# VectorE's attention as a hardware loop, and 160 matmuls that reuse the weights already held

## The chip, the cores and the metric

One core of one Trainium2 chip. The metric is the device time of one execution in microseconds (us); the quoted number is the median of the fast runs. Runs in a slow state, over 1.5% above the fastest of the same kernel, are left out (for the kernel before these were 888.3 us once and about 444 us in single runs). The traces' own span is about 1.3 us shorter than the measured time.

## The reference, cut to what matters

```python
mod = (_silu(c) @ w_mod).reshape(c.shape[0], 6, 1, -1)       # six shifts, scales, gates
h = _layernorm(x, axis=-1) * (1 + ca) + sa
q = (h @ wq) ...                                             # 8 rows, 32 heads of 128
scores = einsum('bhqd,bhkd->bhqk', q, k) * Dh ** (-0.5)      # k_cache: 8 x 4 x 8192 x 128
o = einsum('bhqk,bhkd->bhqd', softmax(scores), v)            # v_cache: the same size
x = x + ga * (o @ wo)
h = _layernorm(x, axis=-1) * (1 + cb) + sb
x = x + gb * ((relu(h @ W_gate) * (h @ W_up)) @ W_down)
```

One token for each of 8 batch entries attends to 8192 cached keys and values. The two caches are 134 MB, and all inputs together about 186 MB. Each byte is used once, so this is a streaming kernel.

## The kernel before

The attention is 16 tiles (`M = 16`). A tile is one K and one V load of 4.19 MB each. The loads go through a ring in on-chip memory with room for four of them. A small scheduler records every operation with what it reads and writes, works out the waits, and emits one program per engine. TensorE's attention was already a hardware loop of 8 trips with two tiles each; VectorE's was written out 16 times.

```python
def pump():                              # issues the next load when its place in the ring is free
    while stream:
        key, src, n = stream[0]
        lo = cursor[0] if cursor[0] + n <= RING else 0
        if P.unread("arena", lo, lo + n):
            return
        ...
        P.op("sp", lambda e, dst=dst, src=src: e.dma_start(dst, src), writes=[slot_r(lo, lo + n)], dma=True, ...)

def qk_part(m, e8):                      # scores of an eighth of a tile: 4 matmuls
    ...
    P.op("pe", fns, reads=[R("kt", to, to + QE), R("qpad", ...), slot_r(place["k", m] + e8 * QE, ...)], writes=[bank(b)])

for m in range(M):
    P.trip = m // 2
    for e8 in range(8):
        kt_part(m, e8)                   # VectorE: transposes an eighth of K (ring of 4 results)
        qk_part(m, e8)                   # TensorE: scores of that eighth
        if e8 == 5:
            rowmax(m, 0)                 # VectorE: maximum of the first half
    make_qpad(m + 2)                     # GpSimd: padded queries for a later tile
    fold(m - 1, 0); fold(m - 1, 1)       # VectorE: gathers the output of the tile before
    rowmax(m, 1); spread(m); fold(m - 1, 2)
    headmax(m)                           # VectorE: maximum of each head -> bias
    expo(m)                              # ScalarE: exponentials
    fold(m - 1, 3); fold_pe(m - 1); ...
    p_turn(m)                            # VectorE: transposes the probabilities
    pv(m)                                # TensorE: 32 matmuls, probabilities times V
```

In the modulation, query, gate and up stages 4 column tiles (`tile_position=(0, 32 * j)`) multiply the same `hT[:, kk, :]` by two or three blocks of columns. Each matmul loaded these weights anew.

## Time and profile before

| | before |
|---|---|
| time, median of the fast runs | 437.71 us |
| span in the trace | 436.2 us |
| bytes moved | 185.63 MB |
| busy: TensorE, VectorE | 63%, 60% |
| weight loads | 1697 |

From the page of the kernel before: the busy row, then the share of the DMA engines and the GB/s in 40 equal slices of the span, then the load queue.

```profile
PE 273.5 (63%) x1697; PEld 124.0 (28%) x1697; DVE 263.0 (60%) x373; ACT 30.7 (7%) x65; POOL 20.9 (5%) x79
...
DMA  9999999999999999999999999999999999999995
GB/s 376 421 457 431 433 433 431 430 433 433 433 433 433 433 433 433 433 433 433 433 433 433 433 433 433 433 433 433 433 433 430 433 433 433 441 429 434 427 421 224
...
q1 hardware_dynamic: 6848, 185.63, 98.8%
```

The DMA engines are full in every slice but the last, at 433 GB/s. 185.63 MB at 433 GB/s are 428.7 us of the 436.2.

The chain that ended last in the kernel before, by engine and by line:

```profile
DMA 38%; PE 33%; DVE 20%; issue 8%; ACT 0%; SPq 0%
DMA arena<-in_A_k_cache_dram 25%; PE ps L594 13%; PE ps L550 12%; DVE kt L539 12%; DMA arena<-in_w_mod_dram 7%; DMA arena<-in_B_W_down_dram 6%; DVE negm L558 4%; PE ps L744 2%; PE ps L694 1%; PE ps L564 1%; PE ps L615 1%; DVE om L609 1%; DVE mj L569 1%; PE ps L725 1%; PE ps L463 1%
```

VectorE's longest wait in the kernel before (total us, times, longest):

```profile
DVE kt L539 <- DMA arena<-in_A_k_cache_dram: 37.9, 16, 3.1
```

And the load queue's own waits, for a place in the ring:

```profile
SPq L343 <- PE ps L594: 182.0, 16, 12.7
SPq L343 <- PE ps L550: 127.1, 16, 16.9
```

V's place is freed by the PV matmuls (L594), K's by the score matmuls (L550). How far ahead the loads run is in the last column of the issue lines (KB each, median us from issue to landing):

```profile
arena<-in_A_k_cache_dram SPq DMA_DIRECT2D x16, 4096.0 KB, 27.5
arena<-in_A_v_cache_dram SPq DMA_DIRECT2D x16, 4096.0 KB, 25.6
```

One such load takes 4.19 MB / 433 GB/s = 9.7 us, so at its issue there is a queue in front of it. The order of one tile in the timeline of the kernel before (start us, duration, engine, line, operation):

```profile
220.09 5.38 PE L550 MATMUL ps<-kt,qpad 128*128 128x512 bf16 x24
220.19 0.33 SPq L343 DMA_DIRECT2D arena<-in_A_v_cache_dram  x1
...
223.80 0.66 DVE L558 TENSOR_REDUCE negm<-ps 128x1 f32<-128x512 f32 x1
...
227.87 0.33 SPq L343 DMA_DIRECT2D arena<-in_A_k_cache_dram  x1
```

V's load goes out as soon as the PV matmuls end (220.19), and K's as soon as the last score matmul ends (227.87).

One stage with weight loads to be removed, the second query batch, as a window of the kernel before (window; busy us and count of PE, PEld, DVE, ACT, POOL; granted clock; DMA share; GB/s):

```profile
52.30:56.00 3.70, 3.60 (x32) 1.08 (x32) 0.00 (x0) 0.00 (x0) 0.00 (x0) 0.50 0.98 425
```

### The profile page before, as it was taken

Reading aid. Unit: us, or ns where it says so; the run is one execution under the profiler, and the core shown is the slowest. Engines: PE = TensorE matmul, PEld = TensorE weight load, DVE = VectorE, ACT = ScalarE, POOL = GpSimd, SP = SyncE. Lnnn points to the kernel's source line nnn. Section 1 sums busy time; section 2 is a strip of 40 time slices with the busy share of each in tenths; the row PEclk is TensorE's granted clock in tenths of the full one; section 3 lists DMA queues with packets and bytes.
Section 4 is the critical chain, followed back from the end, with each engine's and each line's share of the span. In section 5 each row is a group of like instructions: output and inputs, shape, how many; then the busy total and the mean of one; then the engine's idle time right before and its main releaser. Section 6 shows DMA issues by size and latency. Waiting matters only on the chain.

```text
span 436.2 us, 4054 instructions
## 1 busy us (share of the span) xinstructions
PE 273.5 (63%) x1697; PEld 124.0 (28%) x1697; DVE 263.0 (60%) x373; ACT 30.7 (7%) x65; POOL 20.9 (5%) x79
## 2 busy tenths in 40 slices
PE   0052447769595866859586775959586684655237
PEld 0021112324242332424233232423233231342015
DVE  0233057778596878778696877859686877332020
ACT  1100020010101011010101101010101101010000
POOL 7000010000000000000000000000000000000000
PEclk9996558698787989787896969879798978868568
DMA  9999999999999999999999999999999999999995
GB/s 376 421 457 431 433 433 431 430 433 433 433 433 433 433 433 433 433 433 433 433 433 433 433 433 433 433 433 433 433 433 430 433 433 433 441 429 434 427 421 224
DMA packets 6939, 185.79 MB, mean 426 GB/s; under 512 B 816, under 2 KB 912, under 8 KB 1168
## 3 DMA queue, kind: packets, MB, share of 16 engines
q1 hardware_dynamic: 6848, 185.63, 98.8%
q8 instruction: 6, 0.10, 0.1%
q10 hardware_dynamic: 80, 0.02, 0.0%
q14 instruction: 5, 0.04, 0.0%
HBM read 185.63 MB, written 0.02 MB: 426 GB/s over the span
## 4 chain that ended last, share of the span: by engine, by line
DMA 38%; PE 33%; DVE 20%; issue 8%; ACT 0%; SPq 0%
DMA arena<-in_A_k_cache_dram 25%; PE ps L594 13%; PE ps L550 12%; DVE kt L539 12%; DMA arena<-in_w_mod_dram 7%; DMA arena<-in_B_W_down_dram 6%; DVE negm L558 4%; PE ps L744 2%; PE ps L694 1%; PE ps L564 1%; PE ps L615 1%; DVE om L609 1%; DVE mj L569 1%; PE ps L725 1%; PE ps L463 1%
## 5 line engine op out<-in xcount | busy, mean ns | idle before, releaser
L539 DVE STREAM_TRANSPOSE kt<-arena 128x1024 uint32<-128x1024 uint32 x128 | 148.5, 1214 | 40.5 <-DMA arena<-in_A_k_cache_dram 37.9
L550 PE MATMUL ps<-kt,qpad 128*128 128x512 bf16 x512 | 122.0, 384 | 10.3 <-DVE kt L539 8.8
L594 PE MATMUL ps<-arena,pT 128*64 128x512 bf16 x512 | 92.0, 538 | 50.9 <-issue 50.9
L594 PEld LDWEIGHTS ps<-arena,pT 128*64 128x64 bf16 x512 | 44.2, 153 | 92.6 <-issue 86.7
L550 PEld LDWEIGHTS ps<-kt,qpad 128*128 128x128 bf16 x512 | 45.6, 97 | 85.2 <-DVE kt L539 29.6
L585 DVE STREAM_TRANSPOSE pT<-prb 64x1024 bf16<-64x1024 bf16 x32 | 39.7, 1239 | 16.8 <-ACT prb L578 16.3
L578 ACT ACTIVATE prb<-ps,bias 128x1024 bf16<-128x1024 f32 x16 | 17.8, 1114 | 286.5 <-DVE mjt L572 286.5
L558 DVE TENSOR_REDUCE negm<-ps 128x1 f32<-128x512 f32 x32 | 22.0, 688 | 11.3 <-PE ps L550 11.1
L532 POOL COPY qpad<-qR 32x32 bf16<-32x32 bf16 x64 | 13.0, 203 | 304.7 <-PE ps L550 252.0
L725 PE MATMUL ps<-arena,hT 128*32 128x448 bf16 x128 | 11.0, 515 | 13.6 <-DMA arena<-in_B_W_gate_dram 6.8
L564 PE MATMUL ps<-identf,negm 128*128 128x128 f32 x32 | 7.8, 326 | 15.6 <-DVE negm L562 15.6
L615 PE MATMUL ps<-jmp,om 128*128 128x16 f32 x34 | 6.7, 273 | 16.9 <-DVE om L609 16.1
L609 DVE SCALAR_TENSOR_TENSOR om<-ps,im,om 128x128 f32<-128x128 f32 x48 | 16.7, 347 | 0.6
L486 PE MATMUL ps<-arena,hT 128*32 128x512 bf16 x64 | 7.2, 631 | 14.1 <-DMA arena<-in_A_wq_dram 14.1
L732 DVE TENSOR_TENSOR kt<-ps,kt 128x448 bf16<-128x448 f32 x2 | 1.2, 620 | 23.5 <-PE ps L725 23.5
L744 PE MATMUL ps<-arena,hmT 128*32 128x256 bf16 x112 | 9.0, 332 | 5.3 <-DMA arena<-in_B_W_down_dram 5.3
L401 DVE CAST cxr<-ps 128x512 bf16<-128x512 f32 x1 | 0.7, 692 | 18.1 <-PE ps L399 18.1
L399 PE MATMUL ps<-cx,rsel 32*128 32x512 bf16 x1 | 0.6, 604 | 17.5 <-DMA cx<-in_c_dram 17.5
L564 PEld LDWEIGHTS ps<-identf,negm 128*128 128x128 f32 x32 | 4.7, 186 | 23.5 <-DVE negm L562 23.5
L496 DVE CAST kt<-ps 128x512 bf16<-128x512 f32 x1 | 0.7, 692 | 17.8 <-PE ps L486 17.8
L615 PEld LDWEIGHTS ps<-jmp,om 128*128 128x128 f32 x34 | 5.1, 188 | 20.3 <-DVE om L609 19.4
L725 PEld LDWEIGHTS ps<-arena,hT 128*32 128x32 bf16 x128 | 4.2, 128 | 20.1 <-DMA arena<-in_B_W_gate_dram 7.2
(89 smaller groups left out, 103.9 us busy)
## 6 DMA issues: line engine op xcount, KB each, us to landing
arena<-in_A_k_cache_dram SPq DMA_DIRECT2D x16, 4096.0 KB, 27.5
arena<-in_A_v_cache_dram SPq DMA_DIRECT2D x16, 4096.0 KB, 25.6
arena<-in_w_mod_dram SPq DMA_DIRECT2D x2, 6144.0 KB, 24.0
arena<-in_A_wq_dram SPq DMA_DIRECT2D x2, 4096.0 KB, 31.1
arena<-in_A_wo_dram SPq DMA_DIRECT2D x2, 4096.0 KB, 26.9
arena<-in_B_W_gate_dram SPq DMA_DIRECT2D x2, 3584.0 KB, 23.6
arena<-in_B_W_up_dram SPq DMA_DIRECT2D x2, 3584.0 KB, 24.6
arena<-in_B_W_down_dram SPq DMA_DIRECT2D x1, 3584.0 KB, 25.5
```

The costliest lines, as they stand in the source:

```text
L532: P.op("pool", lambda e, n=2 * m + Q // 2, Q=Q: e.tensor_copy(qpad[32 * Q:32 * Q + 32, m % 2, :, 24 + 32 * Q:32 + 32 * Q], qR[32 * Q:32 * ...
L539: P.op("dve", lambda e: e.transpose(ktb[:, to:to + QE].bitcast(dt.uint32), arena[:, lo:lo + QE].bitcast(dt.uint32)), reads=[slot_r(lo, lo ...
L550: fns.append(lambda e, t=t, r=r: e.matmul(ps[:, b, :].rearrange("p (c k) -> p c k", k=32), qpad[:, m % 2, t * 2 + r, 24 - 8 * i:152 - 8 * ...
L558: P.op("dve", lambda e: e.tensor_reduce(negm[:, h:h + 1], ps[:, b, :], AX.X, ALU.max, negate=True), reads=[bank(b)], writes=[R("negm", h, ...
L564: P.op("pe", lambda e: e.matmul(ps[:, 4, 0:128], negm[:, 2:3].to_broadcast([128, 128]), identf[:], start=True, stop=True), reads=[R("negm" ...
L578: P.op("act", lambda e: e.activation(prb[:], ps[:, 2 * z:2 * z + 2, :].rearrange("p h n -> p (h n)"), ACT.Exp, bias=bias[:, z:z + 1], scal ...
L585: P.op("dve", lambda e, g=g: e.transpose(pT[64 * g:64 * g + 64, z, :, g, :], prb[64 * g:64 * g + 64, :]), reads=[R("prb"), R("pT", z, z + ...
L594: fns.append(lambda e, t=t: e.matmul(ps[64 * (t % 2):64 * (t % 2) + 64, 5, :].rearrange("p (i d) -> p i d", d=Dh), pT[:, z, t].rearrange(" ...
L609: P.op("dve", lambda e, i=i: e.scalar_tensor_tensor(out=om[:], in0=ps[:, 5, Dh * i:Dh * i + Dh], scalar=im[:, i:i + 1], in1=om[:], op0=ALU ...
L615: P.op("pe", lambda e: e.matmul(ps[:, 6 + z, 0:16], om[:], jmp[:].rearrange("p g j -> p (g j)"), start=True, stop=True), reads=[R("om"), R ...
L725: fns.append(lambda e, w=w, r=kk - r0, kk=kk, h=h, j=j, b0=b0: e.matmul(ps[32 * j:32 * j + 32, b0 + h, 0:H], hT[:, kk, :], w[:, r, j, h, : ...
L744: fns.append(lambda e, w=w, r=k - r0, k=k, i2=i2, j=j: e.matmul(ps[32 * j:32 * j + 32, 4, 0:256], hmT[:, k, 1 - i2:33 - i2], w[:, r, i2, j ...
```

## The change

The intent is a shorter program for VectorE, and fewer weight loads on TensorE. A loop can only wait for counts that rise by the same amount on every trip, so the change also moves where a load finds out that its place is free. Its core, with cuts marked by `...`:

```diff
+    LOOPED = ("dve", "pe")
...
-                with nc.Fori(0, len(self.trips), engines=(mybir.EngineType.PE,)):
+        with nc.Fori(0, len(self.trips["pe"]), engines=tuple(kinds[x] for x in self.LOOPED)):
...
+def hold_weights(nc, held):
+    names = {x.ins.name for x in held}
+    for block in nc.main_func.blocks:
+        block.instructions = [copy.replace(x, ldweights=False) if x.name in names else x for x in list(block.instructions)]
...
-                            start=(kk == 0), stop=(kk == KC - 1), tile_position=(0, 32 * j)))
+                            start=(kk == 0), stop=(kk == KC - 1), tile_position=(0, 32 * j)), pr > 0))
... (the same for the query with z > 0, for gate and up with h > 0)
-            P.op("pe", fns, reads=[R("kt", to, to + QE), R("qpad", m % 2, m % 2 + 1), slot_r(place["k", m] + e8 * QE, ...)],
+            P.op("pe", fns, reads=[R("kt", to, to + QE), R("qpad", m % 2, m % 2 + 1)],
...
+        def free(*keys):
+            return [slot_r(*P.held.pop(key)) for key in keys if key in P.held]
...   (rowmax)
-                 reads=[bank(b)], writes=[R("negm", h, h + 1)])
+                 reads=[bank(b)] + (free(("v", m - 1)) if h == 0 else []), writes=[R("negm", h, h + 1)])
...   (headmax)
-                 reads=[R("mj"), R("jms")], writes=[R("mjt"), R("bias", z, z + 1)])
+                 reads=[R("mj"), R("jms"), R("qpad", z, z + 1)] + free(("k", m)), writes=[R("mjt"), R("bias", z, z + 1)])
...   (order of the tile)
-            make_qpad(m + 2)
             fold(m - 1, 0)
...
             headmax(m)
+            make_qpad(m + 2)
```

Two query copies also change places between VectorE and ScalarE. `fold(-1, ...)` now runs in the first tile instead of a memset, so that all trips are alike.

## The prediction

> **What bounds the kernel now.** The DMA stream. The page's 40 slices show the DMA engines at nine tenths or more in 39 slices and 430 to 433 GB/s nearly throughout attention. The DMA queues moved 185.63 MB: at 433 GB/s that is 428.7 us of a 436.2 us span; the rest is start-up (376 GB/s in the first slice) and the tail. The Trainium skill, "DMA: Bandwidth & Descriptors", section "Where 436 GB/s comes from", gives 435.2 GB/s as the ceiling of the 16 SBUF ports; the measured 433 agrees. TensorE (63% busy) and VectorE (60%) are not the limit, although the chain of waits names them (PE 33%, DVE 20%): in the list of waits VectorE waits 37.9 us for K tiles, 2.4 us in each of 16 half-trips.
>
> **Removed.**
> 1. 160 weight loads (64 modulation, 32 query, 64 gate/up), about 0.15 us each by the profile but overlapping matmuls: in the query stage (timeline, granted clock 0.50) four loads take 0.16 us in a pitch of 0.43 us, which the matmuls set. These stages shorten by at most 1 us together. All end before the next DMA lands; the tightest is up's second half, whose product is ready 2.3 us before the down weights land (422.4 against 424.7). On the critical path: 0.
> 2. VectorE's 16 half-trips of program text become 2 in a loop of 8. Executed instructions stay about 373.
>
> **Added or moved.**
> 1. A register update and compare-and-branch per trip on VectorE. Estimate 0.1 to 0.5 us a trip, before a transpose where VectorE waits 1.9 to 2.7 us for K anyway. "Runtime: NRT & Kernel Launch", "Instruction fetch mechanics", warns that a taken branch outside the fetch window stalls; TensorE's existing loop shows none (0.41 us before the first score matmul, at trip ends as within trips).
> 2. Loads wait for VectorE alone. K's slot is freed by the head-max step instead of the last score matmul: about 2 us later. V's is freed by the next tile's first row-max instead of the last PV matmul: 4.3 us later (220.2 to 224.5 in the timeline). Loads now land a median of 27.5 us (K) and 25.6 us (V) after issue, while 4.19 MB takes 9.7 us: 16 to 18 us of earlier transfers are still queued at issue. The delays eat slack; the stream stays unbroken. First tiles are tightest (about 8 us left). Issue-to-landing medians should fall to about 25.5 and 21.5 us, GB/s unchanged.
> 3. The query copies swap between VectorE and ScalarE; the first K lands 2.7 us after they end. GpSimd's padding copies start 2 us later, a whole tile before use.
>
> **On the critical path:** nothing. Start, stream and tail (last down tile, two VectorE operations, output DMA: about 3 us) are untouched.
>
> **Predicted: 437.6 us, 80% range 436.9 to 438.5.** Faster by over 2%: 1%; within 2%: 97%; slower by over 2%: 2%.
>
> **What would show each step right:** 433 GB/s in the attention slices; weight loads 1537, not 1697; VectorE's busy time within 1 us; the load queue waiting for VectorE lines instead of TensorE lines; V issue-to-landing about 4 us shorter; VectorE still waiting for K in most half-trips, its loop ends hidden there.
>
> **What would make it wrong:** an instruction-fetch stall of over 5 us at each of VectorE's loop ends (fetches share the saturated DMA engines); a late slot release that empties the queue, most likely at the first V reloads or the second gate tile (about 9 us of slack); a lower granted clock in the down projection, where TensorE is just ahead of the DMA (waits of 0.26 and 0.30 us), costing up to 1 us; matmuls without their load running slower than with it.

## The result, and the profile after

| | before | after |
|---|---|---|
| time, median of the fast runs | 437.66 us | 437.19 us |
| fast over fast | | 0.9987, 95% interval 0.9972 to 1.0002 |
| span in the trace | 436.2 us | 435.9 us |
| instructions in the trace | 4054 | 3952 |

A ratio is the mean time of one kernel's fast runs over the mean of the other's of the same rounds. It need not be the ratio of the medians, because a mean feels a single long run. The verdict is "same": 0.5 us between the medians, and an interval that just includes 1.

From the page of the kernel after, the lines shown of before:

```profile
PE 275.6 (63%) x1697; PEld 120.4 (28%) x1537; DVE 265.4 (61%) x376; ACT 30.7 (7%) x65; POOL 20.9 (5%) x79
...
DMA  9999999999999999999999999999999999999995
GB/s 367 435 447 436 432 433 433 432 430 433 433 433 433 433 433 433 431 433 433 433 433 433 433 433 433 433 431 433 433 433 433 433 433 433 426 433 444 421 425 233
...
q1 hardware_dynamic: 6848, 185.63, 98.9%
```

The same stream with the same 433 GB/s, and 160 weight loads fewer.

The chain that ended last in the kernel after:

```profile
PE 46%; DVE 20%; issue 13%; DMA 7%; ACT 0%; SPq 0%
PE ps L634 21%; PE ps L586 18%; DVE kt L575 9%; DMA arena<-in_B_W_down_dram 7%; DVE negm L598 5%; PE ps L604 2%; PE ps L651 2%; PE ps L762 1%; PE ps L731 1%; DVE om L645 1%; DVE mj L609 1%; DVE mjt L612 1%; DVE negm L602 1%; DVE kt L721 0%; DVE lx L693 0%
```

The chain's share of loads fell from 38% to 7%, while the time did not move. A chain that changes its face this much at equal time may mean that two limits lie side by side. It is weak evidence: the wait for K has another name in the kernel after (see below), and the chain of `loop_only`, which has the same loop and waits, adds up to only 18% of the span. The experiments below decide.

VectorE's wait for K in the kernel after. `DVEq` is VectorE's own sequencer: it waits for the load and counts its semaphore back down, so the wait is the former wait for K under another name.

```profile
DVE kt L575 <- DVEq L180: 30.6, 16, 2.8
```

The load queue's waits:

```profile
SPq L377 <- DVE negm L598: 204.4, 15, 14.4
SPq L377 <- DVE mjt L612: 94.8, 16, 19.2
```

The load issues:

```profile
arena<-in_A_k_cache_dram SPq DMA_DIRECT2D x16, 4096.0 KB, 25.0
arena<-in_A_v_cache_dram SPq DMA_DIRECT2D x16, 4096.0 KB, 20.7
```

And the same tile in the timeline of the kernel after:

```profile
221.15 5.38 PE L586 MATMUL ps<-kt,qpad 128*128 128x512 bf16 x24
...
224.84 0.69 DVE L598 TENSOR_REDUCE negm<-ps 128x1 f32<-128x512 f32 x1 [0.23 <-PE ps L586]
...
225.56 0.33 SPq L377 DMA_DIRECT2D arena<-in_A_v_cache_dram  x1
...
230.94 0.33 SPq L377 DMA_DIRECT2D arena<-in_A_k_cache_dram  x1
```

V's load now waits for the row maximum, 4.4 us after the PV matmuls end. K's waits for the head maximum. So loads land 2.5 us (K) and 4.9 us (V) sooner after their issue: less of a queue in front of them, and none of it lost to the stream.

The second query batch, as a window of the kernel after:

```profile
52.90:56.60 3.70, 3.60 (x32) 0.59 (x16) 0.03 (x1) 0.03 (x1) 0.00 (x0) 0.50 1.07 461
```

Half of the weight loads are gone, and the 32 matmuls take 3.60 us as before, at the same granted clock of 0.50. The loads had been hidden behind the matmuls.

### The profile page after: what moved, and what is told of

The parts are those of the page before. It is cut to its first block, busy times and chain, and to the rows that moved or that the text cites. A ratio compares the mean times of both kernels' runs of the same rounds, so it can differ in the third digit from the quotient of the medians.

```text
span 435.9 us, 3952 instructions
## 1 busy us (share of the span) xinstructions
PE 275.6 (63%) x1697; PEld 120.4 (28%) x1537; DVE 265.4 (61%) x376; ACT 30.7 (7%) x65; POOL 20.9 (5%) x79
## 4 chain that ended last, share of the span: by engine, by line
PE 46%; DVE 20%; issue 13%; DMA 7%; ACT 0%; SPq 0%
PE ps L634 21%; PE ps L586 18%; DVE kt L575 9%; DMA arena<-in_B_W_down_dram 7%; DVE negm L598 5%; PE ps L604 2%; PE ps L651 2%; PE ps L762 1%; PE ps L731 1%; DVE om L645 1%; DVE mj L609 1%; DVE mjt L612 1%; DVE negm L602 1%; DVE kt L721 0%; DVE lx L693 0%
## 5 line engine op out<-in xcount | busy, mean ns | idle before, releaser
L575 DVE STREAM_TRANSPOSE kt<-arena 128x1024 uint32<-128x1024 uint32 x128 | 149.6, 1217 | 36.8 <-DVEq L180 30.6
L586 PE MATMUL ps<-kt,qpad 128*128 128x512 bf16 x512 | 121.8, 384 | 9.5 <-DVE kt L575 8.2
L634 PE MATMUL ps<-arena,pT 128*64 128x512 bf16 x512 | 93.1, 543 | 50.8 <-issue 50.8
L625 DVE STREAM_TRANSPOSE pT<-prb 64x1024 bf16<-64x1024 bf16 x32 | 39.7, 1239 | 16.7 <-ACT prb L618 16.1
L598 DVE TENSOR_REDUCE negm<-ps 128x1 f32<-128x512 f32 x32 | 22.1, 692 | 12.2 <-PE ps L586 12.2
L568 POOL COPY qpad<-qR 32x32 bf16<-32x32 bf16 x64 | 13.1, 204 | 307.7 <-DVE mjt L612 254.3
L762 PE MATMUL ps<-arena,hT 128*32 128x448 bf16 x128 | 12.3, 570 | 10.8 <-DMA arena<-in_B_W_up_dram 5.5
L645 DVE SCALAR_TENSOR_TENSOR om<-ps,im,om 128x128 f32<-128x128 f32 x51 | 17.7, 347 | 0.7
L435 PE MATMUL ps<-cx,rsel 32*128 32x512 bf16 x1 | 0.6, 604 | 17.7 <-DMA cx<-in_c_dram 17.7
L781 PEld LDWEIGHTS ps<-arena,hmT 128*32 128x32 bf16 x112 | 6.0, 109 | 9.2 <-DMA arena<-in_B_W_down_dram 8.1
## 6 DMA issues: line engine op xcount, KB each, us to landing
arena<-in_A_v_cache_dram SPq DMA_DIRECT2D x16, 4096.0 KB, 20.7
```

The costliest lines, as they stand in the source:

```text
L568: P.op("pool", lambda e, n=2 * m + Q // 2, Q=Q: e.tensor_copy(qpad[32 * Q:32 * Q + 32, m % 2, :, 24 + 32 * Q:32 + 32 * Q], qR[32 * Q:32 * ...
L575: P.op("dve", lambda e: e.transpose(ktb[:, to:to + QE].bitcast(dt.uint32), arena[:, lo:lo + QE].bitcast(dt.uint32)), reads=[slot_r(lo, lo ...
L586: fns.append(lambda e, t=t, r=r: e.matmul(ps[:, b, :].rearrange("p (c k) -> p c k", k=32), qpad[:, m % 2, t * 2 + r, 24 - 8 * i:152 - 8 * ...
L598: P.op("dve", lambda e: e.tensor_reduce(negm[:, h:h + 1], ps[:, b, :], AX.X, ALU.max, negate=True), reads=[bank(b)] + (free(("v", m - 1)) ...
L625: P.op("dve", lambda e, g=g: e.transpose(pT[64 * g:64 * g + 64, z, :, g, :], prb[64 * g:64 * g + 64, :]), reads=[R("prb"), R("pT", z, z + ...
L634: fns.append(lambda e, t=t: e.matmul(ps[64 * (t % 2):64 * (t % 2) + 64, 5, :].rearrange("p (i d) -> p i d", d=Dh), pT[:, z, t].rearrange(" ...
```

## The experiments

Twelve kernels ran. All passed the comparison with the reference, also the four that are meant to compute something else: its tolerance doesn't notice their cuts, so passing says nothing about them.

### Which part moved the half microsecond

`hold_only` is the kernel before with only the weights held, `loop_only` the kernel after with every weight load put back, and `after_again` the kernel after unchanged. All ran on one chip in the same rounds.

```diff
  # hold_only: the kernel before, plus
+        hold_weights(nc, holding)          # and hold(...) around the matmuls of the four stages
  # loop_only: the kernel after, with
-        if when:
+        if False:
             holding.append(ins)
```

> The kernel before with only the weights held (160 loads fewer); VectorE straight, slots freed as before. The whole change came out about 0.5 us faster than before, less than 0.2 per cent. Theory A (instruction fetches: the traces show 6 fetches of 16 KB on one queue before and 5 after, 5 against 3 of 8 KB on another, each carried in 0.9 or 0.3 us, and loads land when the slowest DMA engine is done): 5 of the 16 KB fetches and 5 of the 8 KB fetches here, and most of the gain, 437.1 to 437.5 us. Theory B (the gain comes from the loop or the later slot release): no gain, 437.5 to 437.8. In both the time stays within 0.3 per cent of before, because the stream bounds it.

> The kernel after with all weight loads put back (1697 loads); VectorE's loop and the later slot release kept. Theory A: 6 fetches of 16 KB and 3 of 8 KB, so part of the gain at most, 437.3 to 437.7 us. Theory B: the whole gain, 437.0 to 437.3. V loads land about 21 us after issue as in the kernel after.

> The kernel after, unchanged, in the same rounds: 437.0 to 437.3 us, 0.3 to 0.6 us under before, as in the first measurement. If the difference from before is not there in these rounds, it was a matter of the day and nothing needs explaining.

| | time | ratio to before |
|---|---|---|
| before | 437.65 us | |
| hold_only | 437.58 us | 0.9978, 0.9923 to 1.0033 |
| loop_only | 436.86 us | 0.9966, 0.9917 to 1.0015 |
| after_again | 437.05 us | 0.9964, 0.9915 to 1.0013 |

Before had three fast runs of 438.3 to 444.0 us in these rounds, which widens all intervals; read the medians. Holding the weights gave nothing (0.07 us). The kernel with the loop alone gave all of it (0.8 us); it has the later release and the swapped query copies too. In theory A, the 16 KB fetches carried most of the gain. That falls: `hold_only` has one of them fewer in its trace (5 instead of 6) and is no faster. Theory B, the loop or what comes with it, stands. What comes with the loop are two fetches fewer of 8 KB (3 instead of 5 during the span). The next two runs ask whether such fetches can cost anything.

### Do instruction fetches cost the stream anything

`pool_pad` and `pool_pad_half` add 1200 and 600 one-element memsets at the end of GpSimd's program. GpSimd is idle then, and nobody waits for it.

```diff
+        padt = sb("padt", [128, 1200], dt.bfloat16)
+        for i in range(1200):              # 600 in pool_pad_half
+            P.op("pool", lambda e, i=i: e.memset(padt[0:1, i:i + 1], 0.0), writes=[R("padt", i, i + 1)])
         P.plan()
```

> The kernel after with 1200 one-element memsets added at the end of GpSimd's program, which is idle then and which nobody waits for: about 77 KB of instructions more to fetch, no other work. Theory A: the fetched bytes hold up one DMA engine of 16 (27 GB/s of 433), so 0.5 to 2.8 us longer than after. Rival (fetches cost only their bytes spread over all engines, 0.18 us, or nothing): within 0.3 us of after.

> Half the dose of the padding: 600 memsets on idle GpSimd, about 4 or 5 fetches of 8 KB more than in the kernel after instead of 9. 1200 cost 4.3 us, about 0.46 us a fetch. If each fetch holds up the one DMA engine that finishes last: 1.7 to 2.4 us over after, about 439.2 us. If the cost sits in something that comes once (another placement in memory, a threshold): 0 or 4 us. The stream's slices before the pads must stay the same.

`pool_pad` took 441.39 us, 4.3 us more than `after_again` in the same rounds. `pool_pad_half` took 438.16 us, about 1.1 us more than `after_again`, which ran on another chip (before read 437.65 us on both). The fast runs of each lie within 0.3 us. The traces count 12 fetches of 8 KB in `pool_pad`, 7 in `pool_pad_half` and 3 in the kernel after.

The DMA rows of `pool_pad` show where the time went:

```profile
DMA  9999999999999999999999999999999999999992
GB/s 408 439 395 429 427 441 450 437 429 429 429 429 429 429 435 429 436 447 441 432 429 429 432 429 429 429 436 432 447 441 433 427 427 427 437 419 429 446 407 89
```

Look at the last slice: 89 GB/s, where the kernel after had 233. Adding up the load packets of the trace in order of their ends, 184 MB had been moved after 427.5 us in the kernel after and after 427.7 us in `pool_pad`. But 185.6 MB took 432.2 and 436.1 us. So the bulk of the stream kept its pace, and a small rest of it came 3.9 us late. The last down tile's weights, and all output behind them, wait for that rest.

The packet and landing records of the traces show where the delay sits. While the stream runs, 16 load packets are in flight; during each added fetch there are 15. From 432.7 to 436.7 us, the end of `pool_pad`'s loads, there is one at a time, each starting as the last one ends, at first 8 KB in 0.31 us: about a sixteenth of 433 GB/s. Each load leaves 16 landing events, which I take as one per DMA engine (the trace does not name the engines). How late the last of the 16 is after the eighth:

| | last load before the pads | after all pads | last load of the stream |
|---|---|---|---|
| after | 1.98 us | 1.96 us | 1.84 us |
| pool_pad_half | 1.74 us | 2.97 us | 2.80 us |
| pool_pad | 2.07 us | 6.28 us | 6.10 us |

One engine fell back, and the others kept their pace. The last landing grew later by 1.2 and 4.2 us, the 1.1 and 4.3 us of the measured times. In `pool_pad` this engine was 3.01, 4.33, 5.63 and 6.28 us late after 4, 6, 8 and 9 of the added fetches, and in `pool_pad_half` 2.97 us after 4: 0.65 us a fetch in both. Reckoned back, it had been 0.4 us late before the pads, while another engine was already 2.07 or 1.74 us late. So the first 1.4 to 1.7 us of delay were free, and the rest cost time in full. That is why four fetches cost 0.28 us each and nine 0.48 us, and why both runs missed the range I had given (more than expected at 1200, less at 600).

The same records explain the half microsecond, as far as one trace of each kernel can:

| | load before 330 us landed | next load landed | last load landed | span |
|---|---|---|---|---|
| before | 323.35 us | 334.00 us | 433.24 us | 436.2 us |
| hold_only | 323.83 us | 333.89 us | 433.13 us | 436.1 us |
| after | 323.83 us | 333.56 us | 432.89 us | 435.9 us |
| after_again | 323.68 us | 333.42 us | 432.75 us | 435.7 us |
| loop_only | 323.38 us | 333.07 us | 432.45 us | 435.4 us |

`before` and `hold_only` have an 8 KB fetch at 330.3 and 330.2 us, and there one engine falls back by 0.96 us. The three kernels with the loop have no fetch there, and their stream ends earlier. The 16 KB fetches are not free either: in the kernel after, the one at 46.2 us put an engine back from 0.58 to 2.10 us, about the lag with which the last engine ends. In these traces it is not the number of fetches that counts, but whether they fall on the engine that ends last.

GpSimd paid as well. From 337 us on it stood still for 1.2 us after every 128 memsets, each time just after a fetch (at 340.5 and 346.0 us here); that it waits for the fetch is not shown:

```profile
342.20 4.27 POOL L797 MEMSET padt<- 1x1 bf16 x128 [1.23 <-issue]
347.68 4.27 POOL L797 MEMSET padt<- 1x1 bf16 x128 [1.21 <-issue]
```

### Does the stream alone bound attention

`less_pv` runs 4 of the 32 PV matmuls of a tile. `before_light` and `after_light` cut each K and V load to a quarter of its columns. `both_light` has both cuts. All four leave work out, and so compute something else.

```diff
  # before_light, after_light, both_light
-                dst = arena[:, lo:lo + n]
+                q = n // 4 if key[0] in "kv" else n
+                dst = arena[:, lo:lo + q]
...              (the source is cut to the same columns)
  # less_pv, both_light
-            for t in range(32):
+            for t in (0, 1, 30, 31):
```

> The kernel after with 4 of the 32 PV matmuls of every tile (wrong result on purpose): about 80 us of TensorE's 275 us of busy time gone, and the V slot is freed no earlier than VectorE lets it. If the stream bounds: within 0.5 us of after. If TensorE or the chain through PV bounds attention, as the chain of waits suggests (PE 46 per cent), 10 us or more faster.

> The kernel before with each K and V load cut to a quarter of its columns (wrong result on purpose; the rest of the tile holds old data). The stream no longer binds in attention: I expect a tile to take about 17 us instead of 19.3, and about 385 to 402 us in all, DMA busy share in attention about 0.3.

> The same cut in the kernel after. Here VectorE's loop ends are not hidden by waits for K. My estimate of 0.1 to 0.5 us a trip gives 1 to 4 us more than the cut kernel before. Rival 1 (loop ends stall for instruction fetch): more than 8 us more. Rival 2 (the loop is free also where VectorE bounds): within 0.5 us. If the held weights are worth anything, it shows here only in the head and the tail, which are still bound by loads.

> The kernel after with both cuts at once: a quarter of each K and V load, and 4 of 32 PV matmuls. Either cut alone gave little (10 us; nothing). If the stream (19.37 us a tile) and the alternation of TensorE and VectorE (19.3 us a tile in the cut-load kernels) are two separate limits of nearly the same length, both cuts together must give much more than the sum: in the run with fewer PV matmuls a tile takes VectorE 17.0 us from the first transpose to the last probability transpose without its wait for K, so a tile of about 17.0 us and about 388 to 398 us in all. If instead something else holds the tile at 19.3 us, about 426 us again.

| | time | one tile, from transposes' starts |
|---|---|---|
| after_again | 437.05 us | 19.4 us (in the trace of after) |
| less_pv | 437.16 us | 19.4 us |
| before_light | 428.29 us (426.31 to 430.65) | 19.4 us |
| after_light | 426.83 us (426.05 to 427.78) | 19.4 us |
| both_light | 391.73 us (390.32 to 394.23) | 17.0 us |

The tile's length is the mean distance between the first transposes of the third and the last tile, divided by the 13 tiles between. `less_pv` did as the stream theory said: PV work was taken away, and nothing was gained. (TensorE's busy time fell by 40 us and not by the 80 expected: PV lost 76 us, but the score matmuls took 154.1 us instead of 121.8.)

But the cut loads did not. I had expected 385 to 402 us, and 101 MB fewer bytes bought only 9 us. In attention the DMA moved about 100 GB/s, yet a tile took as long as before. The GB/s of `before_light`, and VectorE's longest wait in it:

```profile
GB/s 372 446 419 443 411 283 88 86 124 99 99 99 99 106 91 160 47 188 99 99 99 99 99 99 123 75 194 31 171 99 99 99 345 327 419 390 304 431 420 234
...
DVE kt L540 <- PE ps L551: 33.4, 15, 2.9
```

The 37.9 us that VectorE had waited for K became 33.4 us of waiting for TensorE. The transposed eighths of K go through a ring of four, so the fifth waits for a score matmul, and the score matmuls wait behind the PV matmuls. This alternation of the two engines takes 19.4 us a tile by itself. The stream takes 8.39 MB / 433 GB/s = 19.4 us. There are two limits of nearly the same length.

`both_light` confirms it. Each cut alone gave 0 or about 10 us; together they gave 45 us, at the 17.0 us a tile that I had worked out for VectorE without its waits. VectorE's transposes in `both_light`, two tiles:

```profile
211.62 6.88 DVE L576 STREAM_TRANSPOSE kt<-arena 128x1024 uint32<-128x1024 uint32 x6
...
228.69 6.88 DVE L576 STREAM_TRANSPOSE kt<-arena 128x1024 uint32<-128x1024 uint32 x6
```

Now six transposes run in one go with no wait before them, and the next tile starts 17.07 us later.

### What a loop end costs where nothing hides it

`after_light` answers this too, since no wait for K stands at its tile ends. In its timeline the first pair of lines is inside a trip, the second across a loop end:

```profile
229.23 2.51 DVE L626 STREAM_TRANSPOSE pT<-prb 64x1024 bf16<-64x1024 bf16 x2 [1.01 <-ACT prb L619]
231.77 4.62 DVE L576 STREAM_TRANSPOSE kt<-arena 128x1024 uint32<-128x1024 uint32 x4
...
247.76 2.51 DVE L626 STREAM_TRANSPOSE pT<-prb 64x1024 bf16<-64x1024 bf16 x2 [1.01 <-ACT prb L619]
250.31 4.62 DVE L576 STREAM_TRANSPOSE kt<-arena 128x1024 uint32<-128x1024 uint32 x4
```

231.77 - 229.23 - 2.51 = 0.03 us inside, and 250.31 - 247.76 - 2.51 = 0.04 us across. Unrounded, all 15 gaps of this trace are 0.03 us, and those of `before_light`, which has no VectorE loop, too. My estimate of 0.1 to 0.5 us a trip was too high; the loop end cost nothing visible, and `after_light` is no slower than `before_light`.

### How far the later release was from breaking the stream

These release the ring's places later still: V by the next tile's head maximum (`late_v`), in addition K by the next tile's first row maximum (`late_kv`), or both by the next tile's head maximum (`later_kv`).

```diff
  # late_v (late_kv: free(("v", m - 1)) here, ("k", m - 1) in rowmax; later_kv: ("k", m - 1), ("v", m - 1) here)
-  ... R("qpad", z, z + 1)] + free(("k", m)), writes=[R("mjt"), ...
+  ... R("qpad", z, z + 1)] + free(("k", m), ("v", m - 1)), writes=[R("mjt"), ...
-  reads=[bank(b)] + (free(("v", m - 1)) if h == 0 else []), writes=[R("negm", h, h + 1)])
+  reads=[bank(b)], writes=[R("negm", h, h + 1)])
```

> The kernel after with V's slot freed still later, by the next tile's head-max instead of its first row-max (about 5.4 us later). V issue-to-landing falls from 20.7 to about 15 us, which is still over the 9.7 us of one transfer plus about 1.5 us to start: time unchanged within 0.4 us of after, 430 to 433 GB/s in attention. If the stream is more fragile than I think, it lengthens by more than 2 us.

> K's slot freed by the next tile's first row-max (13 us later than in the kernel after) and V's by the next tile's head-max. K issue-to-landing about 11.5 us, at the edge: K's landing follows its issue by 11.2 us, and issue follows the landing of K before by about 8.7 us, so a tile takes about 19.9 us instead of 19.35: 437 to 447 us, DMA slices a few per cent under 433 GB/s.

> K's and V's slots both freed by the next tile's head-max, so that two tiles' loads are issued together with the queue drained. K lands about 13.5 + 11.2 = 24.7 us after K before: 5.3 us a tile more, 505 to 525 us. This is what it would look like if the later release of the change had cut into the stream; the change itself stops 6 to 9 us short of it.

| | time | K, V: issue to landing | one tile |
|---|---|---|---|
| after | 437.19 us | 25.0, 20.7 us | 19.4 us |
| late_v | 437.35 us | 25.3, 16.0 us | 19.4 us |
| late_kv | 460.35 us | 13.1, 17.7 us | 20.8 us |
| later_kv | 532.22 us | 12.2, 21.5 us | 25.6 us |

`late_v` came out as expected: another 5 us later, no loss. `late_kv` and `later_kv` broke the stream as the theory said but cost more than the ranges I had given (437 to 447 and 505 to 525 us). The GB/s of `late_kv`:

```profile
GB/s 410 418 413 453 417 453 415 372 410 410 415 390 441 410 413 405 407 418 330 450 332 441 427 418 398 404 408 390 421 398 450 330 424 364 456 403 440 441 410 240
```

This is what a broken stream looks like: no row of 433s, and holes down to 330. The step of my estimate that was off shows in the timeline of `later_kv`, where K's load goes out with the queue empty:

```profile
300.21 0.33 SPq L377 DMA_DIRECT2D arena<-in_A_k_cache_dram  x1
```

The next tile's first transpose starts at 312.57 us in that trace: 12.4 us after the issue. I had taken 9.7 us for the transfer and 1.5 us to start, 11.2 us; the second term is 2.7 us. That makes 1.2 us a tile, over some 14 tiles 17 us.

## Why the prediction was right

**The time.** 437.6 us was predicted with a range of 436.9 to 438.5, and 437.19 us was measured. "On the critical path: nothing" held to within the 0.5 us between the medians.

**Weight loads.** Right: 1537 instead of 1697, worth 0.07 us in `hold_only`, with the matmuls of the query's second batch at 3.60 us with and without them.

**The later release.** Right in mechanism and nearly in size: 25.0 and 20.7 us from issue to landing, predicted about 25.5 and 21.5. `late_v` shows that slack was left, `late_kv` where it ended. "16 to 18 us of earlier transfers are still queued" overstates the reserve, because a load needs 12.4 us by itself and not 9.7.

**The loop end.** Right that it would cost nothing, for a better reason than I gave. I said that the wait for K would hide 0.1 to 0.5 us; it is 0.03 us, as inside a trip, also where no wait hides it. The Trainium skill, "Runtime: NRT & Kernel Launch", section "Instruction fetch mechanics", warns of stalls at branches out of the fetch window; no trace here shows one.

**VectorE's busy time within 1 us.** Missed: 263.0 to 265.4 us. Of the 2.4 us, the K transposes give 1.1 (149.6 against 148.5 us) and the folds 1.0 (17.7 against 16.7 us; three more run, in the first tile). But `loop_only`, with the same loop and folds, shows 263.1 us in all, so most of it is a difference between runs. Nothing followed from it.

**"TensorE (63% busy) and VectorE (60%) are not the limit, although the chain of waits names them."** This step failed. I read VectorE's 2.4 us of waiting for K in each tile as slack against the engines. With three quarters of the K and V bytes taken away, a tile still took 19.4 us, and the wait turned into one for TensorE. The chain of waits had been right to name both. The prediction survived since the change made neither limit longer: the alternation of TensorE and VectorE kept its length, and the stream its pace. In this step that was luck, since nothing in the prediction looked at the second limit. Had I used this step to predict an experiment with less data, I would have been far off, and with `before_light` I was: by 26 us from the nearer end of my range.

**The half microsecond.** I had predicted no change. That the loop gives 0.6 to 0.8 us is at the edge of the noise. The explanation that the runs support is one fetch fewer on the DMA engine that ends last: the padding runs show that a fetch of 8 KB puts one engine back by 0.65 us, and the traces show the gap between the kernels opening at the fetch at 330 us that the loop does away with. The prediction had named fetches only as a stall of VectorE, and not as a delay of the loads. That this one fetch is the whole gain was not tested alone: `loop_only` has the later release and the swapped copies too. `late_v`, which releases V another 5 us later, is no faster than the kernel after (437.35 us).

## What to carry to other kernels

Before calling one resource the limit, cut its work and see whether the time follows; a wait on it in every step only says that it comes last, maybe by a hair. When two limits tie, each cut alone shows nothing, and only cutting both together does. A stream spread over 16 DMA engines ends with its latest engine, so even a small transfer on that one counts. A change off the critical path still has a budget to keep: here V's release could move by some 9 us for free, and moving K's by 13 us on top of that cost 23 us.

## What the Trainium skill lacked or had wrong

- "Runtime: NRT & Kernel Launch", section "Instruction fetch mechanics", calls the cost of crossing a fetch boundary mostly hidden. Here the stream of loads paid for it: each fetch of 8 KB put one DMA engine back by 0.65 us, and 4 more of them cost 1.1 us and 9 cost 4.3 us, on an engine that nobody waited for. GpSimd itself stood still for 1.2 us after every 128 memsets, once for each fetch. The page speaks only of 16 KiB blocks; the traces show packets of 16 KB on one queue and of 8 KB on another.
- "Advanced Engine Details and Errata", section "Control Flow Timing", gives about 108 ns for a compare-and-branch. On VectorE the gap across a loop end is 0.03 us, as inside a trip; the page does not say that a branch can be hidden behind the instructions still running.
- "DMA: Bandwidth & Descriptors", section "Where 436 GB/s comes from", says that the HBM side binds HBM-to-SBUF transfers at about 358 GB/s, half of what two cores share. For one core alone this does not hold: this kernel's loads from HBM keep 433 GB/s, near the fabric's 435.2 GB/s that the same section gives. The section itself mentions a measured 425 GB/s.
